# Sliding-window attention: values of two query blocks in one run of matmuls, exponentials of 1024 columns

## The chip, the cores and the metric

The kernel runs on one core of a Trainium2 chip. The metric is the device time of one execution in microseconds (us). The kernel before takes 730.66 us (median of three runs, 730.52 to 731.07). The engines of the core are named as in the profile: PE (TensorE, matmuls) with PEld (its weight loads), DVE (VectorE), ACT (ScalarE), POOL (GpSimd) and SP (SyncE, which issues all transfers here).

## The reference

Attention with 32 heads of 16 dimensions and a causal window of 256 keys stands beside an MLP on the same normalised input, and the output gates one with the other:

```python
xn = layernorm(x)                                  # x: 2048 tokens x 512
q, k, v = split(xn @ wqkv)                         # 32 heads x 16
scores = q k^T * 16 ** -0.5
mask = (i - j >= 0) & (i - j < 256)
s = softmax(where(mask, scores, -1e9)) @ v @ wo
h = gelu(layernorm(xn) @ w1 + b1)                  # 512 -> 1792
g = silu(h @ w2 + b2)
out = x + s * g
```

## The kernel before, in words

**Tiling.** The 2048 tokens are 16 blocks of 128 (qb for queries, kb for keys). The heads are done four at a time: 8 head groups n, so 128 steps of one block of one head group. A query block sees three key blocks: its own (lower triangle), the one before (whole) and the one two before (upper triangle, strict). Products that need precision are made of three products of a high and a low part.

**Slots.** The main loop (line 926) runs over slots t. The slots from -16 to -1 make the inputs ready. Slot t from 0 to 127 does, for step t = 16n + kb: the scores with keys as rows and queries as columns (`prob_block`, line 615, once for each pair of heads p), their exponential on ACT, and two selections on POOL that clear the triangles. It also does the values of step t - 1 (`pv_step`, line 637), and the row maxima of step t + 12 (`LEAD`), which are subtracted through extra rows of q and k before the exponential.

**Scores and exponentials.** One `prob_block` writes 384 columns (its key block against three query blocks) for two heads in two PSUM banks, the tile `stb`, and one ACTIVATE of 2 x 384 = 768 columns reads them. There is one such tile, so the next scores wait until that exponential has ended. In the last 12 slots, where no maxima are left to make, the tile `xy` serves in turn with it.

**Maxima.** `max_block` (line 562) writes the scores of a query block against the block before and its own into `xy` (256 columns for each of four heads), and `first_scores` (line 553) those against the block two before into `zo` (128 columns each). DVE copies the latter over the masked part of the own block (COPY_PREDICATED, 512 elements), and one TENSOR_REDUCE of 1024 elements gives the maxima. `max_rows` (line 584) turns four blocks of them into rows and sends them to the extra rows of q by way of DRAM.

**Values.** `pv_step` multiplies three key blocks' probabilities by v for four heads, each head in a column group of 32 of the PE array, into `otb`, 128 columns of the second bank of `zo`. Each such fp32 matmul is two records in the trace, so a step is 24 records. ACT, in 20 slots DVE, copies `otb` to `oraw`; every fourth step a transfer of 256 KB sends it to DRAM.

**Filling work.** Between these stand units of other matmuls, in the banks `fb`: projections of q, k and v for later head groups, and the first products of the MLP. `tandem` (line 499) makes two jobs run at once, one on the upper and one on the lower 64 rows of the PE array, in two phases between which the two banks change rows. A unit is a pair of matmuls of 512 columns (256 for v). A tandem of q and k has 24 units over five or six slots. Its two results are copied out by ACT at the slot that ends it. `places` deals the units to slots (t, 0) and (t, 1), before and after the slot's second `prob_block`.

**Order.** All engines run their instructions in the order of the program. That order is written by hand: `fills` (units), `plan` by `at(t, ...)` (splits, casts, transfers within a slot), `ends` by `behind(t, ...)` (at a slot's end), and a few tables by slot number such as `MAX_BEHIND` (line 912). Transfers within the slots are issued by SP in that order too. A slot is, in PE's order: scores of p = 1; maxima scores; units; scores of p = 0; units; first scores of the next step; values of the step before.

Of the kernel before, what the change touches and what calls it, by code (L numbers as in the profile page):

```python
# [9 lines left out]
F32 = mybir.dt.float32  # L10
# [40 lines left out]
def mixer_kernel(ctx, tc, x, wqk, wv, wo, w1, b1, w2, b2, out):  # L51
# [12 lines left out]
    pp = attn.enter_context(tc.tile_pool(name="pp", bufs=8))  # L64
# [119 lines left out]
    otb = zo[:, 1, 256:384]  # L184
# [30 lines left out]
    mhalf = const.tile([P, 4], F32, name="mhalf")  # L215
    negc = const.tile([P, 1], F32, name="negc")
# [7 lines left out]
    nc.vector.memset(negc, NEG)  # L224
    mask = upper.bitcast(I32).unsqueeze(1).unsqueeze(1).to_broadcast([P, 2, 2, P])
    neg = negc.unsqueeze(2).unsqueeze(2).to_broadcast([P, 2, 2, P])
    b1s = const.tile([P, NF], F32, name="b1s")
    scales = const.tile([P, 512], F32, name="scales")
# [57 lines left out]

    stage = {}
# [3 lines left out]
    IN_PLACE = (LEAD,)  # L291
# [174 lines left out]
    taken, ends_pair = set(), set()  # L466
# [32 lines left out]
    def tandem(t0, t1, one, two, mid=None, back=None):  # L499

        n = one[0]
        lo, hi = slice(0, 64), slice(64, P)
        mid = mid or max(1, (t0 + t1 + 1) // 2)
        most = n // 4

        def places(slots, last):

            last = min(most, n // (len(slots) + 1)) if last else 0  # L510
            cuts = [(n - last) * k // len(slots) for k in range(len(slots) + 1)]
            out = []
            for t, a, b in zip(slots, cuts, cuts[1:]):
                ahead = min(b - a, n // 3) if t < 16 * NQ - LEAD else min(b - a, max(most, (b - a + 1) // 2))
                out += [(t, 0)] * ahead + [(t, 1)] * (b - a - ahead)
            return out + [(t1, 0)] * last

        first, second = places(range(t0, mid), False), places(range(back or mid, t1), True)
        for phase, where in enumerate((first, second)):
            for i in range(n):  # L520
                flags = dict(start=(phase == 0 and i == 0), stop=(phase == 1 and i == n - 1), skip_group_check=True)
                def unit(i=i, phase=phase, flags=flags):
                    made = ((two if phase == 0 else one)[1](fb[1 - phase], i, hi, **flags),
                            (one if phase == 0 else two)[1](fb[phase], i, lo, **flags))
                    if phase == 1 and i == 0 and t0 < 16 * NQ - LEAD:
                        for r in made:
                            tc.add_manual_dep(r.ins, outs["copy"].ins.name, ORDER, reason="the banks change rows")
                fills.setdefault(where[i], []).append((unit, ()))
        fills.setdefault((t1, 0), []).append((one[2], (fb[0], t1, nc.scalar.copy)))
        if t1 >= 16 * NQ - LEAD:  # L530
            fills[t1, 0].append((two[2], (fb[1], t1, nc.vector.tensor_copy)))
            return
        ends_pair.add(t1)

        def copy(dst, src):
            outs["second"] = nc.scalar.copy(dst, src)
        fills.setdefault((t1, int(t1 + 1 < 16 * NQ - LEAD)), []).append((two[2], (fb[1], t1, copy)))
# [15 lines left out]
    def first_scores(n, qb):  # L553

        slot = slots[n % 2]
        for p in range(2):
            for a in (1, 0):
                r = slice(64 * a, 64 * a + 64)
                nc.tensor.matmul(zo[:, a, P * p: P * (p + 1)], slot[r, 0, p, P * qb: P * (qb + 1)],
                                 slot[r, 1, p, P * (qb - 2): P * (qb - 1)], start=True, stop=True)  # L560

    def max_block(n, qb, ahead=False):

        slot = slots[n % 2]
        if qb % 4 == 0:
            mts[n, qb // 4] = small.tile([P, 2, 2, 4], F32, tag="mt", name=f"mt_{n}_{qb}")
        lo = max(qb - 1, 0)
        off = 128 * (lo + 1 - qb)
        for p in range(2):
            for a in (1, 0):  # L570
                r = slice(64 * a, 64 * a + 64)
                nc.tensor.matmul(xy[:, a, 256 * p + off: 256 * (p + 1)], slot[r, 0, p, P * qb: P * (qb + 1)],
# [869 lines left out]
```

## Time and profile before

| | |
|---|---|
| median of three runs | 730.66 us (730.52 to 731.07) |
| span of the profiled execution | 729.3 us |
| granted TensorE clock | 0.999 |
| PE | 718.0 us busy, 7584 matmul records |
| DVE | 496.2 us busy |
| ACT | 427.6 us busy |
| POOL | 324.1 us busy |

Busy time is the union of an engine's instructions. In a row of the grouped views, the numbers behind the bar are the busy time in us and the mean ns of one instruction, then the idle time of the engine just before them and what ended it. A row of the timeline has the start in us, the duration in us, the engine, the operation, output <- inputs, the shape and how many instructions were merged. Starts of matmuls are recorded, their ends are modelled, and matmuls overlap in the pipeline, so the distance from one start to the next is read rather than the duration. All instructions carry line 43, a helper's, so groups are told apart by tile names: `stb` scores for the exponentials, `pt` probabilities, `zo<-pt` values, `xy` and `zo<-qk` maxima scores, `fb` units, `mt` maxima.

### The profile page before, as it was taken

What the parts mean: (1) busy time and instruction counts of PE and PEld (TensorE: products, weight loads), DVE (VectorE), ACT (ScalarE), POOL (GpSimd) and SP (SyncE); (2) the same over time, 40 slices, a digit from 0 to 9 for tenths busy, and PEclk for the clock granted to TensorE, in tenths of its full rate; (3) what the DMA queues carried; (4) which work ended last, traced back from release to release, by engine and by line L of the source; (5) the groups of instructions that cost most, each with busy time, mean ns of one, the idle gap of its engine ahead of it and who ended that gap; (6) DMA issues with size and microseconds to landing.
All of it is one profiled execution on the core that took longest, in us unless ns stands there. A gap on an engine that the chain in (4) does not pass through costs nothing.

```text
span 729.3 us, 19068 instructions
## 1 busy us (share of the span) xinstructions
PE 718.0 (98%) x7584; PEld 586.6 (80%) x7584; DVE 496.2 (68%) x730; ACT 427.6 (59%) x724; POOL 324.1 (44%) x683
## 2 busy tenths in 40 slices
PE   8999999999999999999999999999999999999997
PEld 8998777777778887777776788888888888888886
DVE  7886776877766777777882656446687856667823
ACT  8767777877777676888878735232344734541001
POOL 7444767767677665777877540203203000001102
PEclk9999999999999999999999999999999999999999
DMA  8324447777776733667624367347223312263701
GB/s 295 81 49 110 100 122 182 219 227 225 199 198 181 209 122 98 161 167 205 179 92 162 104 230 217 129 131 244 87 58 116 117 58 87 68 192 108 249 19 58
DMA packets 61528, 106.77 MB, mean 146 GB/s; under 512 B 12096, under 2 KB 12352, under 8 KB 61440
## 3 DMA queue, kind: packets, MB, share of 16 engines
q1 hardware_dynamic: 61440, 105.56, 49.2%
q8 instruction: 60, 0.98, 0.6%
q14 instruction: 28, 0.23, 0.1%
HBM read 54.53 MB, written 33.82 MB: 121 GB/s over the span
## 4 chain that ended last, share of the span: by engine, by line
PE 93%; ACT 3%; DVE 1%; DMA 1%; SPq 1%; issue 1%; POOL 0%; DVEq 0%; POOLq 0%
PE acc L43 21%; PE fb L43 20%; PE zo L43 14%; PE p L43 9%; PE stb L43 9%; PE s L43 6%; PE h L43 6%; PE xy L43 5%; ACT pt L43 2%; PE pv L43 2%; DVE xy L43 1%; SPq L43 1%; DMA x<-in_x_dram 1%; DVE mt L43 0%; PE tr L43 0%
## 5 line engine op out<-in xcount | busy, mean ns | idle before, releaser
L43 POOL TENSOR_SCALAR_AFFINE_SELECT pt<-pt 128x256 f32<-128x256 f32 x480 | 193.7, 428 | 95.5 <-ACT pt L43 89.4
L43 ACT ACTIVATE pt<-stb 128x768 f32<-128x768 f32 (+1 forms) x244 | 188.8, 774 | 43.2 <-PE stb L43 36.9
L43 DVE TENSOR_REDUCE mt<-xy 128x4 f32<-128x1024 f32 (+1 forms) x128 | 152.6, 1192 | 4.4
L43 DVE COPY_PREDICATED xy<-upper,zo 128x512 f32<-128x512 int32 x112 | 77.9, 695 | 72.1 <-PE xy L43 65.3
L43 POOL TENSOR_TENSOR xo<-xo,gated 128x512 f32<-128x512 f32 x15 | 20.0, 1332 | 221.3 <-DVE gated L43 220.3
L43 PE MATMUL zo<-pt,vt 128*17 128x128 f32 x2880 | 103.7, 275 | 0.0
L43 PE MATMUL fb<-xnT,wqb 64*128 64x512 f32 (+2 forms) x732 | 100.3, 381 | 0.1
L43 PE MATMUL stb<-qk 64*128 64x384 f32 (+1 forms) x488 | 94.6, 382 | 4.6 <-ACT pt L43 2.9
L43 PE MATMUL acc<-w,gh 128*128 128x512 f32 x320 | 98.6, 389 | 0.0
L43 PEld LDWEIGHTS stb<-qk 64*128 64x128 f32 x488 | 45.7, 183 | 48.2 <-ACT pt L43 39.6
L43 PEld LDWEIGHTS zo<-pt,vt 128*17 128x17 f32 x2880 | 67.5, 97 | 15.0 <-issue 4.6
L43 PEld LDWEIGHTS acc<-w,gh 128*128 128x128 f32 x320 | 60.1, 188 | 12.5
L43 PEld LDWEIGHTS fb<-xnT,wqb 64*128 64x128 f32 (+1 forms) x732 | 62.6, 185 | 6.7 <-DVE xy L43 0.3
L43 PE MATMUL acc<-w,gl 128*128 128x512 f32 x160 | 62.2, 389 | 0.0
L43 PE MATMUL xy<-qk 64*128 64x256 f32 (+2 forms) x536 | 57.7, 289 | 0.2 <-DVE mt L43 0.2
L43 PE MATMUL p<-xnT 128*128 128x512 f32 x189 | 51.8, 389 | 0.0
L43 ACT COPY oraw<-zo 128x128 f32<-128x128 f32 x108 | 28.8, 266 | 37.4 <-PE zo L43 28.8
L43 PEld LDWEIGHTS xy<-qk 64*128 64x128 f32 x536 | 46.7, 185 | 4.8 <-issue 2.2
L43 ACT ACTIVATE gated<-acc 128x512 f32<-128x512 f32 x16 | 8.7, 596 | 61.9 <-DVE acc L43 61.9
L43 PE MATMUL s<-wos,ohl 128*128 128x512 f32 (+1 forms) x204 | 44.3, 376 | 0.0
L43 PEld LDWEIGHTS s<-wos,ohl 128*128 128x128 f32 x204 | 36.8, 188 | 7.1
L43 PEld LDWEIGHTS p<-xnT 128*128 128x128 f32 x189 | 35.5, 188 | 7.4
(207 smaller groups left out, 1195.5 us busy)
## 6 DMA issues: line engine op xcount, KB each, us to landing
qk<-sh SPq DMA_DIRECT2D x128, 128.0 KB
qk<-pjr SPq DMA_DIRECT2D x64, 128.0 KB
oT_d<-oraw SPq DMA_DIRECT2D x32, 256.0 KB
w_d<-in_w_dram SPq DMA_DIRECT2D x14, 512.0 KB
xt_d<-xnT SPq DMA_DIRECT2D x12, 512.0 KB
x<-in_x_dram SPq DMA_DIRECT2D x16, 256.0 KB
w<-w_d SPq DMA_DIRECT2D x16, 256.0 KB
or<-oT_d SPq DMA_DIRECT2D x16, 256.0 KB
```

The source lines that it names most:

```text
L43: r = issue(*args, **kwargs)
```

## The change

Two slots become one pair u (slots 2u and 2u + 1, key blocks kb and kb + 1 with kb even).

- **Scores** (`prob_part`): three parts per pair, each of 2 x 512 columns with one exponential of 1024. Parts 0 and 1 hold, for head pair p = 0 or 1, key block kb against three query blocks (384 columns) and key block kb + 1 against its own (128). Part 2 holds key block kb + 1 against the two later query blocks (256) for both head pairs. POOL's selections become one of 512 elements and one of 256 for parts 0 and 1, one of 512 for part 2. Seven buffers of 2 x 512 replace eight of 2 x 384.
- **Values** (`pv_part`): once per pair, into 256 columns, with moving operands of 256, 128, 256 and 128 columns; 32 records instead of 2 x 24. One copy of 256 columns, always on ACT, and one transfer of 128 KB per pair.
- **Maxima**: `xy` now holds the two blocks at the ends of the window, own and two before, and `zo` the middle one. DVE overwrites in `xy`, and reduces middle and ends apart (two reductions of 512). `max_rows` joins them with one more small operation on DVE. In the even slot the order is end scores, middle scores, copy, middle reduction, end reduction; in the odd slot the middle scores and their reduction stand behind the scores of part 2, and the end scores behind two thirds of the units.
- **Units**: every tandem now begins at an even slot and takes all of its slots evenly, all ahead of the second place; between the phases PE drains and counts a semaphore, for which the second phase's first unit waits. The second copy of a tandem stands behind the next part 0.
- **Around it**: some steps of the plan move by one or two slots; the scales live in the space of `wa` and are loaded a third time after the slots; `first_h(1)` is multiplied by them later, on POOL; one piece of x is loaded to another pool.

The core of the diff (`max_ends` keeps the old way for the first two blocks of a head group):

```diff
-    pp = attn.enter_context(tc.tile_pool(name="pp", bufs=8))
+    pp = attn.enter_context(tc.tile_pool(name="pp", bufs=7))
...
-    otb = zo[:, 1, 256:384]
+    otb = zo[:, 1, 256:512]
+    mids = zo[:, :, 0:256].rearrange("q a (p k) -> q a p k", p=2)
+    ends_of = xy.rearrange("q a (p e k) -> q a p e k", p=2, e=2)
...
+    def mark():
+        nc.tensor.drain().then_inc(rows_done, 1)
+        marks[0] += 1
+    def follow(made):
+        for r in made:
+            r.wait_op(rows_done, marks[0], "sem-ge")
...
+        def places(slots):
+            cuts = [n * k // len(slots) for k in range(len(slots) + 1)]
+            return [(t, 0) for t, a, b in zip(slots, cuts, cuts[1:]) for _ in range(b - a)]
+        first, second = places(range(t0, mid)), places(range(back or mid, t1 + 1))
...
+                    if phase == 0 and i == n - 1:
+                        mark()
+                    if phase == 1 and i == 0:
+                        follow(made)
...
+        else:
+            fills.setdefault((t1, 2), []).append((two[2], (fb[1], t1, nc.scalar.copy)))
...
+        own = ends_of[:, :, :, 1]
+        outs["max"] = nc.vector.copy_predicated(own, mask, ends_of[:, :, :, 0]),
+        return lambda: nc.vector.tensor_reduce(out=mt, in_=own, axis=AX.X, op=ALU.max, negate=True)
+    def max_middle(n, qb):
+        if qb < 2:
+            return
+        _, mu = max_places(n, qb)
+        for p in range(2):
+            for a in (1, 0):
+                max_scores(mids[:, a, p], n, qb, a, p, lambda row: row[:, P * (qb - 1): P * qb])
+        nc.vector.tensor_reduce(out=mu, in_=mids, axis=AX.X, op=ALU.max, negate=True)
...
+        if part < 2:
+            w = min(384, S - P * kb)
+            for a in (1, 0):
+                scores(128, a, part, kb, kb, w)
+            for a in (1, 0):
+                scores(0, a, part, kb + 1, kb + 1, 128)
+            w += 128
+        else:
+            w = 512
+            for p in range(2):
+                for a in (1, 0):
+                    scores(256 * p, a, p, kb + 1, kb + 2, 256)
+        outs["exp"] = nc.scalar.activation(pt[:, :, 0:w], both[:, :, 0:w], AF.Exp, scale=DH ** -0.5)
...
+        seq = [(kb, lambda j: pts[u, j // 2][:, j % 2, 128:384], 0, 256),
+               (kb + 1, lambda j: pts[u, j // 2][:, j % 2, 0:128], 128, 256)]
+        if kb:
+            seq[:0] = [(kb - 1, lambda j: pts[u - 1, 2][:, j % 2, 256 * (j // 2): 256 * (j // 2 + 1)], 0, 256),
+                       (kb - 2, lambda j: pts[u - 1, j // 2][:, j % 2, 384:512], 0, 128)]
...
+        oraw = sgp.tile([P, 256], F32, tag="or", name=f"oraw_{u}", bufs=2)
+        outs["copy"] = nc.scalar.copy(oraw, otb)
...
+    for u in range(end // 2):
+        t = 2 * u
+        prob_part(u, 1)
+        rest = own_max(max_ends, t + LEAD)
+        own_max(max_middle, t + LEAD)
+        rest()
+        fill_in(t, 0)
+        planned(t)
+        fill_in(t, 1)
+        ended(t)
+        t += 1
+        prob_part(u, 2)
+        own_max(max_middle, t + LEAD)
+        todo = fills.get((t, 0), [])
+        n = sum(fn.__name__ == "unit" for fn, _ in todo)
+        now[:] = t, 0
+        run(delayed.pop((t, 0), ()))
+        for fn, args in todo[:n - n // 3]:
+            fn(*args)
+        planned(t)
+        fill_in(t, 1)
+        own_max(max_ends, t + LEAD)()
+        for fn, args in todo[n - n // 3:]:
+            fn(*args)
+        if t + 1 < end:
+            prob_part(u + 1, 0)
+        fill_in(t, 2)
+        pv_part(u)
+        own_rows(t + LEAD, t)
+        ended(t)
```

More of the change, by code (lines that the diff above doesn't have):

```diff
@@ L503, in tandem @@
         n = one[0]
[L504 to L518, printed above, removed]
+        lo, hi, box = slice(0, 64), slice(64, P), []
+        mid = mid or (t0 + t1 + 1) // 2
+        def places(slots):
+            cuts = [n * k // len(slots) for k in range(len(slots) + 1)]
+            return [(t, 0) for t, a, b in zip(slots, cuts, cuts[1:]) for _ in range(b - a)]
+        first, second = places(range(t0, mid)), places(range(back or mid, t1 + 1))
         for phase, where in enumerate((first, second)):
@@ L556, in first_scores @@
         for p in range(2):
             for a in (1, 0):
[L558 to L568, printed above, removed]
+                max_scores(ends_of[:, a, p], n, qb, a, p,
+                           lambda row: row.rearrange("d (b k) -> d b k", k=P)[:, qb - 2: qb + 1: 2])
```

213 lines of the change are left out of this document (106 added, 107 removed).

## The prediction

> **What bounds the kernel now.** I read the page's head and its chain first, then the windows by stage, the waits of TensorE, and last the timeline of one slot.
>
> ```profile
> span 729.3 us, 19068 instructions
> PE 718.0 (98%) x7584; PEld 586.6 (80%) x7584; DVE 496.2 (68%) x730; ACT 427.6 (59%) x724; POOL 324.1 (44%) x683
> PE 93%; ACT 3%; DVE 1%; DMA 1%; SPq 1%; issue 1%; POOL 0%; DVEq 0%; POOLq 0%
> ```
>
> TensorE (PE) is busy 98% of the span and is 93% of the chain that ended last, so only what shortens PE's own queue counts. But ends of matmuls are modelled, so bubbles hide in "busy"; I look for them between starts.
>
> ```profile
> core 0: us, PE busy (x) PEld busy (x) DVE busy (x) ACT busy (x) POOL busy (x), PEclk, DMA share, GB/s
> 0.00:63.00 63.00, 60.87 (x660) 56.46 (x662) 49.81 (x93) 47.85 (x87) 32.06 (x64) 1.00 0.51 142
> 63.00:380.00 317.00, 311.81 (x5010) 248.15 (x5008) 234.15 (x291) 241.61 (x409) 226.33 (x534) 1.00 0.61 166
> ```
>
> The slots that the change rewrites run from about 60 to 416 us; in 317 us of them ACT works 242 and DVE 234, both near three quarters. The clock is 1.00 throughout.
>
> ```profile
> PEld stb L43 <- ACT pt L43: 39.6, 150, 0.8
> PE stb L43 <- ACT pt L43: 2.9, 10, 0.4
> PE stb L43 <- DMA qk<-mT_d: 0.6, 1, 0.6
> ```
>
> The weight loads of the probability scores (stb) wait for an exponential 150 times, but mostly the matmuls ahead cover it. DMA hardly holds PE.
>
> ```profile
> 304.45 0.34 PE L43 MATMUL stb<-qk 64*128 64x384 f32 x2
> 304.62 0.34 PE L43 MATMUL zo<-qk 64*128 64x128 f32 x4
> 304.88 0.85 PE L43 MATMUL zo<-pt,vt 128*17 128x128 f32 x24
> 305.69 0.44 PE L43 MATMUL stb<-qk 64*128 64x384 f32 x2
> 305.97 0.40 PE L43 MATMUL xy<-qk 64*128 64x256 f32 x4
> 306.20 1.11 PE L43 MATMUL fb<-xnT,wqb 64*128 64x512 f32 x8
> 307.13 0.35 PE L43 MATMUL stb<-qk 64*128 64x384 f32 x2
> 307.32 0.38 PE L43 MATMUL zo<-qk 64*128 64x128 f32 x4
> 307.63 0.85 PE L43 MATMUL zo<-pt,vt 128*17 128x128 f32 x24
> 308.41 0.44 PE L43 MATMUL stb<-qk 64*128 64x384 f32 x2
> ```
>
> Start to start, this is one slot. Two row halves run at once, so x2 is one pair: 0.23 us for 512 columns (four units in 306.20 to 307.13), 0.12 for 256 (xy), 0.17 for 384 (304.45 to 304.62), hence some 0.06 for 128. That line goes through nothing fixed. Around the values (zo<-pt) it does not hold. Two pairs of 128 before them take 0.26 rather than 0.12: 0.14 to get in.
>
> ```profile
> 65.89 0.41 PE L43 MATMUL zo<-pt,vt 128*17 128x128 f32 x8
> ...
> 68.84 0.63 PE L43 MATMUL zo<-pt,vt 128*17 128x128 f32 x16
> ...
> 379.24 0.41 PE L43 MATMUL zo<-pt,vt 128*17 128x128 f32 x8
> ```
>
> Eight records more cost 0.22, so 24 are 0.66; from 307.63 to 308.41 it is 0.78, 0.12 to get out. The first scores behind take 0.28 (305.69 to 305.97) rather than 0.17, 0.11 more. **One block of values costs 0.37 us beside its columns.** The rows 65.89 and 379.24 are the same block of two head groups 112 slots apart: 313.35/112 = 2.80 us a slot. Without any wait a slot with four units is 0.28+0.23+0.93+0.17+0.26+0.78 = 2.65.
>
> **The change, part by part.** Durations for the other engines:
>
> ```profile
> L43 ACT ACTIVATE pt<-stb 128x768 f32<-128x768 f32 x214 | 174.0, 813 | 38.2 <-PE stb L43 32.1
> L43 ACT ACTIVATE pt<-stb 128x512 f32<-128x512 f32 x15 | 9.0, 599 | 2.7 <-PE stb L43 2.7
> L43 DVE TENSOR_REDUCE mt<-xy 128x4 f32<-128x1024 f32 x120 | 147.1, 1226 | 4.1
> L43 DVE TENSOR_REDUCE mt<-xy 128x4 f32<-128x512 f32 x8 | 5.5, 694 | 0.3
> L43 DVE COPY_PREDICATED xy<-upper,zo 128x512 f32<-128x512 int32 x112 | 77.9, 695 | 72.1 <-PE xy L43 65.3 <-PE zo L43 5.1 <-ACT oraw L43 0.7
> L43 ACT COPY oraw<-zo 128x128 f32<-128x128 f32 x108 | 28.8, 266 | 37.4 <-PE zo L43 28.8 <-POOL mh L43 2.3 <-DVE mT L43 1.9
> L43 ACT COPY vt<-fb 128x256 f32<-128x256 f32 x5 | 1.7, 376 | 3.0 <-PE fb L43 3.0
> L43 ACT COPY pjr<-fb 128x512 f32<-128x512 f32 x26 | 15.3, 590 | 2.8 <-PE fb L43 1.2 <-PE stb L43 0.6
> L43 DVE COPY oraw<-zo 128x128 f32<-128x128 f32 x20 | 5.8, 290 | 1.9 <-PE zo L43 0.5
> L43 DVE TENSOR_TENSOR wqb<-wqkr,wqb 128x512 fp32r<-128x512 f32 x7 | 5.4, 767 | 0.0
> L43 POOL TENSOR_TENSOR hr<-hr,scales 128x512 f32<-128x512 f32 x6 | 7.9, 1345 | 11.0 <-DMA hr<-h_d 11.0
> ```
>
> 1. *Values once per two slots.* 128 blocks become 64: 64 x 0.37 = **-23.7**. Columns stay: 6x128 per slot before, (256+128+256+128) x 2 passes per pair now. Scores stay 1536 columns per pair in six pairs of matmuls instead of four; by the straight line that is 0. [...]
>
> 2. *A pair of slots, hand-timed from the first score pair at 0.* Scores of p=1 (384 and 128 columns) 0.28+0.06 = 0.34; end scores to 0.57; middle scores to 0.69; four units to 1.62; scores of part 2 (two pairs of 256) to 1.85; the odd middle scores to 1.97; three units to 2.67; end scores to 2.90; a unit to 3.13; scores of the next p=0 to 3.36; in 0.14, values 1.32, out 0.12: 4.94 against 2 x 2.65 = 5.30.
>
> ```profile
> 304.83 0.81 ACT L43 ACTIVATE pt<-stb 128x768 f32<-128x768 f32 x1
> 305.85 0.27 ACT L43 COPY oraw<-zo 128x128 f32<-128x128 f32 x1 [0.21 <-PE zo L43]
> 306.17 0.82 ACT L43 ACTIVATE pt<-stb 128x768 f32<-128x768 f32 x1
> 306.46 0.70 DVE L43 COPY_PREDICATED xy<-upper,zo 128x512 f32<-128x512 int32 x1 [0.86 <-PE xy L43]
> ```
>
> 3. *Exponentials.* 256 columns more cost 813-599 = 214 ns, so 1024 take 1.03; three per pair are 3.08 against 4 x 0.813 = 3.25. An exponential starts 0.48 after its scores (305.69, 306.17), here 0.54, and ends at 1.57. PE wants the buffer at 1.62, but a released buffer is used 0.05 later (305.64, 305.69), and a load that had to wait costs the 0.11 again: 1.73, a wait of 0.1. The exponential of the next p=0 lies under the values (1.32), where today's lies under 0.66. Waits today: 2.80 less 2.65 is 0.15 a slot, about 20 us in 128 slots (extra units and the shorter first blocks nearly cancel). New ones of this kind: 0.1 x 64 behind part 1, perhaps 0.14 x 64 elsewhere in the pair, 15. I take **-5**, between -15 (PE always covers) and +5.
>
> 4. *Middle maxima.* The reduction of 1024 (1226) becomes two of 512 (2 x 694); the in-place end block has copy 695 and reduction 694. VectorE's order in an even slot is copy, middles, ends. The end scores start at 0.34, the copy 0.49 later (305.97, 306.46), 0.83 to 1.53; middles to 2.22, ends to 2.91. The odd slot's middle scores overwrite the middles: allowed at 2.22+0.05+0.11 = 2.38, wanted at 1.85+0.1 = 1.95. **A new wait of 0.4**; behind it in PE's queue stand the odd slot's units, end scores and the next scores. Slots with more than four units and phase ends fill part of it; I take 0.3. It is there in 51 pairs (58 pairs still prepare maxima, 7 begin a head group and have no middles): **+15.3**, between 0 and 51 x 0.42 = 21. The odd reductions end well under the values: 0.
>
> 5. *Drains.* 22 row changes of the fill banks now drain PE and count a semaphore, where the first unit used to wait for the values' copy. Nothing in the trace shows a drain; the nearest rows are a matmul's 0.39 less its 0.23 of streaming (1.11 for four units in 0.93) plus the 0.11 of a late load, 0.27 each: 6 at most, 0 at least. 18 stand at the end of an even slot, where items 3 and 4 make PE wait anyway: **+1.5**.
>
> 6. *Copies on ScalarE.* All value copies are now there, 64 of 376 instead of 108 of 266 (and 20 on DVE). At 20 pair ends both bank copies (590 each) and this one stand in a row ahead of the next exponential, and the even middle scores share a bank with the values. With the second copy ahead, the values' copy ends about 0.4 later than PE wants that bank; item 4's wait absorbs most: 0.15 x 20 = **+3**, between 0 and 8. [...]
>
> 7. *The rest.* Before the slots ten blocks have middles: 10 x 0.16 on DVE, 49.81 of 63.00 busy, half exposed: **+0.8** (0 to 2). Selects on GpSimd cover the same elements in 5 instead of 8 instructions, and the values now come a part later: 0. Values leave in 64 transfers rather than 32, 32 more issues on SyncE that nobody waits for: 0. The third load of the scales and one multiply on GpSimd stand under the first matmuls after the slots: 0; uncovered 1.3 for the multiply and the load beside it.
>
> Sum: -23.7 -5 +15.3 +1.5 +3 +0.8 = -8.1. The profiled execution spans 729.3, 1.4 under the median of 730.66; I take the change off the median: **722.6**.
>
> **The rivals.** *PE alone decides (20%).* If PE comes to the odd middle scores no earlier than VectorE, because of the 0.1 waits, drains and extra units, item 4 is nil: 722.6-15.3 = 707.3, with item 3's own waits there some 709. For it: DVE has 25% idle. Against it: the hand schedule misses by 0.4.
>
> *VectorE sets the pace (20%), slower.* Its work per pair grows from 3.84 to 4.17, and any further instruction of it ahead of the even middles (a 0.77 subtraction of a weight, a transpose) adds wholly to PE's wait. It decides from a wait of 0.3+8.1/51 = 0.46 per pair; at 0.6 it is 722.6+15.3 = 737.9. For it: the three in a row are serial and PE's other work there is fixed. Against: nearly nothing else runs on DVE before the last third.
>
> *The waits only move (13%).* If the exponentials cost as much waiting as today and a little more (item 3 at +3 instead of -5), the time is 730.6. For it: three long links on one buffer. Against: the longest cover, the values, doubles.
>
> That fewer blocks are issued is fixed by the program; that each costs 0.37 was seen with and without a wait ahead.
>
> **How the numbers follow.** The forecast itself has 47% (716 to 729). With PE alone 20%, moved waits 13%, VectorE 20%, the range 708 to 735 leaves out the far half of the last and the tail below the first. 0.2% (1.5 us) is about what a measurement of this kernel can tell. Faster 67%, same 13%, slower 20%.
>
> **What would show it.** Right: 64 blocks of 32 records, the 0.14, 0.12 and 0.11 once each per pair; exponentials of 1.03; pairs near 5.4 where four units stand in each slot; PE's load for the odd middle scores waiting for a DVE reduction. Wrong: pairs near 5.05 (PE alone) or above 5.6 (VectorE), 256-column passes of values that take other than 0.22, or drains over 0.3.

## The result

| | before | after |
|---|---|---|
| median of four runs each | 730.85 us (730.52 to 731.07) | 741.04 us (738.69 to 742.74) |
| profiled execution, span | 729.3 us | 737.0 us |
| ratio after / before | | 1.0137, 95% interval 1.0115 to 1.0158 |

The change makes the kernel 1.4% slower: 10.2 us by the medians, 7.7 us by the two profiled spans. The forecast was 722.6 us, faster, with 735 us as the upper end of its range. It is wrong in sign and out of its range.

The head of the page of the kernel after, and the chain that ended last:

```profile
span 737.0 us, 17546 instructions
PE 714.8 (97%) x6848; PEld 574.2 (78%) x6848; DVE 504.4 (68%) x854; ACT 408.5 (55%) x608; POOL 302.8 (41%) x500
PE 87%; ACT 4%; DVE 3%; DMA 2%; issue 2%; SPq 1%; POOL 1%; ACTq 0%; DVEq 0%; POOLq 0%
```

TensorE has 736 records fewer, yet its share of the chain fell from 93% to 87%: waits for ScalarE, VectorE and transfers have come in. The windows by stage, and a third one around the worst place:

```profile
core 0: us, PE busy (x) PEld busy (x) DVE busy (x) ACT busy (x) POOL busy (x), PEclk, DMA share, GB/s
63.00:380.00 317.00, 302.77 (x4276) 230.85 (x4276) 232.28 (x390) 219.78 (x301) 201.69 (x364) 0.99 0.63 164
296.00:312.00 16.00, 13.34 (x160) 9.95 (x160) 9.96 (x16) 8.96 (x12) 9.08 (x16) 0.89 0.65 159
```

In the same 317 us of the slots TensorE is busy 303 us instead of 312, and its clock is no longer 1.00 throughout. Half of the pairs of slots still take 5.5 us or less, near what was drawn by hand. One of them in the timeline of TensorE, start to start:

```profile
203.11 0.51 PE L43 MATMUL stb<-qk 64*128 64x384 f32 x4 [0.59 <-ACT pt L43]
203.45 0.45 PE L43 MATMUL xy<-qk 64*128 64x256 f32 x4
203.86 0.44 PE L43 MATMUL zo<-qk 64*128 64x128 f32 x4
204.14 1.13 PE L43 MATMUL fb<-xnT,wqb 64*128 64x512 f32 x8
205.11 0.39 PE L43 MATMUL stb<-qk 64*128 64x256 f32 x4
205.34 0.38 PE L43 MATMUL zo<-qk 64*128 64x128 f32 x4
205.56 0.90 PE L43 MATMUL fb<-xnT,wqb 64*128 64x512 f32 x6
...
206.77 0.41 PE L43 MATMUL stb<-qk 64*128 64x384 f32 x4
207.11 1.49 PE L43 MATMUL zo<-pt,vt 128*17 128x256 f32 x32
208.54 0.51 PE L43 MATMUL stb<-qk 64*128 64x384 f32 x4
208.87 0.39 PE L43 MATMUL xy<-qk 64*128 64x128 f32 x4
209.10 1.15 PE L43 MATMUL fb<-xnT,wqb 64*128 64x512 f32 x8
210.33 0.51 PE L43 MATMUL stb<-qk 64*128 64x256 f32 x4
```

From 203.11 to 208.54 are 5.43 us; the forecast said near 5.4 where four units stand in each slot. But a look inside shows other terms than it named. The two places with middle scores take 0.28 (203.86 to 204.14) and 0.22 us (205.34 to 205.56), where 0.12 were drawn, and no wait of the forecast's 0.3 stands at the second. That the sum of this pair agrees is luck in part. And the pairs are not all like this one. By the starts of the values' blocks, the 56 pairs from 66.93 to 386.09 us take 5.70 us on average, against two slots of 2.80 before. The longest is this, again in TensorE's timeline:

```profile
298.28 1.49 PE L43 MATMUL zo<-pt,vt 128*17 128x256 f32 x32
299.70 0.50 PE L43 MATMUL stb<-qk 64*128 64x384 f32 x4
302.78 0.44 PE L43 MATMUL xy<-qk 64*128 64x128 f32 x4 [2.58 <-DMA qk<-pjr]
...
304.27 0.69 PE L43 MATMUL stb<-qk 64*128 64x256 f32 x4
304.74 1.50 PE L43 MATMUL fb<-xnT,wqb 64*128 64x512 f32 x6
```

TensorE waits 2.58 us for the low parts of q and k of the next head group (`qk<-pjr`). Behind the wait the clock falls, to 0.50 from 304.5 to 307.5 us: six unit records take 1.50 us, above (205.56) 0.90. The waits of TensorE over the whole span:

```profile
PE stb L43 <- ACT pt L43: 3.8, 9, 0.7
PE xy L43 <- DMA qk<-pjr: 2.6, 1, 2.6
PE stb L43 <- DMA qk<-mT_d: 2.5, 2, 2.1
PE xy L43 <- DVE mt L43: 1.9, 4, 0.8
```

The second and third are about rows of head groups that arrive late: before, `xy` had no such wait, and that for `qk<-mT_d` was 0.6 us. In the part of the forecast on bounds stood "DMA hardly holds PE".

### The profile page after: what moved, and what is told of

Its sections match the earlier page's. It is cut to its first block, busy times and chain, and to the rows that moved or that the text cites. A ratio compares the mean times of both kernels' runs of the same rounds, so it can differ in the third digit from the quotient of the medians.

```text
span 737.0 us, 17546 instructions
## 1 busy us (share of the span) xinstructions
PE 714.8 (97%) x6848; PEld 574.2 (78%) x6848; DVE 504.4 (68%) x854; ACT 408.5 (55%) x608; POOL 302.8 (41%) x500
## 4 chain that ended last, share of the span: by engine, by line
PE 87%; ACT 4%; DVE 3%; DMA 2%; issue 2%; SPq 1%; POOL 1%; ACTq 0%; DVEq 0%; POOLq 0%
PE acc L43 20%; PE fb L43 18%; PE zo L43 13%; PE p L43 9%; PE stb L43 7%; PE s L43 6%; PE h L43 6%; PE xy L43 5%; ACT pt L43 2%; PE pv L43 2%; DVE mt L43 1%; SPq L43 1%; DVE xy L43 1%; DMA qk<-pjr 1%; DMA qk<-mT_d 1%
## 5 line engine op out<-in xcount | busy, mean ns | idle before, releaser
L43 ACT ACTIVATE pt<-stb 128x1024 f32<-128x1024 f32 (+1 forms) x176 | 177.7, 1010 | 72.5 <-PE stb L43 65.2
L43 POOL TENSOR_SCALAR_AFFINE_SELECT pt<-pt 128x512 f32<-128x512 f32 (+1 forms) x296 | 163.5, 573 | 124.4 <-ACT pt L43 123.9
L43 DVE COPY_PREDICATED xy<-upper,xy 128x512 f32<-128x512 int32 x112 | 77.8, 694 | 71.4 <-PE xy L43 71.3
L43 POOL TENSOR_TENSOR xo<-xo,gated 128x512 f32<-128x512 f32 x15 | 20.0, 1331 | 220.1 <-DVE gated L43 219.0
L43 PE MATMUL fb<-xnT,wqb 64*128 64x512 f32 (+2 forms) x732 | 106.1, 390 | 1.2 <-POOL sv L43 1.0
L43 PE MATMUL acc<-w,gh 128*128 128x512 f32 x320 | 98.7, 389 | 1.1 <-ACT gh L43 1.1
L43 DVE TENSOR_REDUCE mt<-xy 128x4 f32<-128x512 f32 (+1 forms) x128 | 92.3, 721 | 2.3
L43 PE MATMUL zo<-pt,vt 128*17 128x128 f32 (+1 forms) x1920 | 90.6, 328 | 0.0
L43 PE MATMUL stb<-qk 64*128 64x384 f32 (+1 forms) x704 | 79.3, 302 | 8.4 <-ACT pt L43 3.8
L43 PEld LDWEIGHTS stb<-qk 64*128 64x128 f32 x704 | 57.5, 186 | 36.2 <-ACT pt L43 18.5
L43 DVE TENSOR_REDUCE mt<-zo 128x4 f32<-128x512 f32 x112 | 76.3, 682 | 1.2 <-PE zo L43 0.7
L43 PEld LDWEIGHTS zo<-pt,vt 128*17 128x17 f32 x1920 | 49.1, 97 | 32.2 <-issue 0.6
L43 PEld LDWEIGHTS acc<-w,gh 128*128 128x128 f32 x320 | 60.0, 188 | 13.8 <-ACT gh L43 1.5
L43 PEld LDWEIGHTS fb<-xnT,wqb 64*128 64x128 f32 (+1 forms) x732 | 62.2, 188 | 7.1 <-POOL sv L43 1.1
L43 PE MATMUL xy<-qk 64*128 64x256 f32 (+2 forms) x544 | 59.0, 294 | 4.7 <-DMA qk<-pjr 2.6
L43 PE MATMUL acc<-w,gl 128*128 128x512 f32 x160 | 62.4, 390 | 0.0
L43 PEld LDWEIGHTS xy<-qk 64*128 64x128 f32 x544 | 45.7, 186 | 12.7 <-issue 4.6
L43 PE MATMUL p<-xnT 128*128 128x512 f32 x189 | 51.8, 389 | 0.0
L43 PE MATMUL zo<-qk 64*128 64x128 f32 x448 | 44.1, 274 | 0.9 <-DVE mt L43 0.2
L43 PE MATMUL s<-wos,ohl 128*128 128x512 f32 (+1 forms) x204 | 44.3, 376 | 0.0
L43 ACT ACTIVATE gated<-acc 128x512 f32<-128x512 f32 x16 | 8.7, 596 | 61.9 <-DVE acc L43 61.9
L43 PEld LDWEIGHTS s<-wos,ohl 128*128 128x128 f32 x204 | 36.8, 188 | 7.1
```

The costliest lines, as they stand in the source:

```text
L43: r = issue(*args, **kwargs)
```

## The experiments

The theories. **1, late rows:** the spans in which q, k and the maxima of the next head group are produced were moved, their transfers come later in SyncE's one ordered queue, and TensorE waits and then runs slow. **2, VectorE's pace:** the wait at the middle maxima. **3, prices:** drains and short matmul steps cost more than forecast, a block of values less.

| kernel | median us | ratio to before | 95% interval |
|---|---|---|---|
| after | 741.04 | 1.0137 | 1.0115 to 1.0158 |
| rows6 | 742.11 | 1.0149 | 1.0136 to 1.0162 |
| mids2 | 738.85 | 1.0100 | 1.0084 to 1.0116 |
| nocp | 736.23 | 1.0069 | 1.0056 to 1.0082 |
| split | 771.85 | 1.0557 | 1.0544 to 1.0571 |
| first | 736.34 | 1.0072 | 1.0050 to 1.0094 |
| oact | 747.35 | 1.0220 | 1.0207 to 1.0233 |
| oact_mids | 739.07 | 1.0109 | 1.0096 to 1.0122 |
| split1 | 762.42 | 1.0436 | 1.0416 to 1.0456 |
| first_nocp | 733.29 | 1.0022 | 1.0004 to 1.0040 |
| drain2 | 746.88 | 1.0217 | 1.0204 to 1.0230 |
| tail | 740.85 | 1.0139 | 1.0125 to 1.0153 |
| best1 | 732.54 | 1.0025 | 1.0015 to 1.0035 |
| before_rows | 735.45 | 1.0066 | 1.0052 to 1.0081 |
| before_short | 737.26 | 1.0084 | 1.0071 to 1.0097 |
| best2 | 730.02 | 0.9991 | 0.9982 to 0.9999 |

Differences between kernels below are differences of ratios times 731 us.

### Late rows: rows6, first, oact, before_rows

**rows6**

```diff
-                               ((76, 81), (82, 87)), ((88, 93), (94, 99))), 2):
+                               ((76, 79), (80, 87)), ((88, 93), (94, 99))), 2):
```

> One change to the kernel after: the rows of head group 6 (its q and k columns after the rotation) are produced at slots 76-79 and 80-87, not 76-81 and 82-87. In the kernel after the group's q and k columns left SyncE at 299.24 us, against 291.17 before, and TensorE waited 2.74 us for them at 299.98 and then ran at half speed for a stretch. Theory 1 (rows that arrive late): this wait goes, with the slow stretch behind it: 3 to 7 us less than the kernel after, so 734 to 738 us, and the pair that took 9.17 us takes 5.5. Theory 2 (VectorE's pace) and theory 3 (drains, and a values block that is cheaper than 0.37 us): within 1 us of the kernel after, since the pairs lose time everywhere and a late row only moves the wait.

Measured: no gain (+0.9 us by the ratios, within the intervals). The wait at 300 us is gone, as theory 1 said, but the time is not. TensorE's waits in the slots of this kernel:

```profile
PE stb L43 <- DMA qk<-mT_d: 5.1, 3, 3.1
```

Waits for the maxima rows (`qk<-mT_d`), 2.5 us in the kernel after, are 5.1 here. So the wait moved to the next late transfer, and one span alone is not the cause. SyncE's issues in the kernel after show what these rows stand behind:

```profile
157.56 1.19 SPq L43 DMA_DIRECT2D qk<-pjr  x2
158.84 0.56 SPq L43 DMA_DIRECT2D mT_d<-mT  x1
159.45 0.56 SPq L43 DMA_DIRECT2D xt_d<-xnT  x1
160.05 0.61 SPq L43 DMA_DIRECT2D wqkr<-in_wqk_dram  x1
160.76 0.76 SPq L43 DMA_DIRECT2D oT_d<-oraw  x1
161.62 0.59 SPq L43 DMA_DIRECT2D qk<-qk  x1
162.30 2.50 SPq L43 DMA_DIRECT2D qk<-sh  x4
164.90 1.43 SPq L43 DMA_DIRECT2D qk<-pjr  x2
166.43 0.55 SPq L43 DMA_DIRECT2D qk<-mT_d  x1
```

Each issue takes SyncE some 0.6 us, and the queue has no gap over 0.2 us. The maxima rows were written out at 158.84, but they are read in at 166.43, behind seven issues for a group that is needed later. TensorE waits for them from 166.47 (168.56 less 2.09):

```profile
166.08 0.39 PE L43 MATMUL fb<-xnT,wqb 64*128 64x512 f32 x2
168.56 0.50 PE L43 MATMUL stb<-qk 64*128 64x384 f32 x4 [2.09 <-DMA qk<-mT_d]
```

**first** (with the edit of rows6)

```diff
-            behind(t + 2, bring_in)
+            at(t + 2, bring_in)
```

> Two changes to the kernel after: the rows of head group 6 are produced at slots 76-79 and 80-87 (as in the run before this one, which by itself brought nothing: the wait at 300 us went, and waits of 2.0 to 3.3 us for the maxima rows stood at 166 and 306 us instead), and SyncE issues the reading-in of the maxima rows at the front of its slot, ahead of the q and k columns of that slot, not behind them. Theory 1 (rows late through SyncE's one ordered queue): with both waits gone and the slow stretch behind each, 4 to 9 us less than the kernel after, 732 to 737 us, and no wait of TensorE on a DMA over 0.5 us between 66 and 385 us. Rival (the late rows are only where a loss shows that VectorE and the blocks make): the waits move once more, 739 to 743 us.

Measured: 4.8 us less than the kernel after, 736.3 us, as theory 1 said. TensorE's wait for `qk<-mT_d` fell to 1.0 us (one place, at 360 us), above the 0.5 that I had set; the wait for `qk<-pjr` is gone. Not all of the gain is the waits themselves: the granted clock was 0.996 to 1.000 in these runs, 0.992 to 0.998 in those of the kernel after. Span times granted clock, an estimate of the time at full clock, is 736.1 us (median) for the kernel after and 733.2 for first, so that some 3 of the 4.8 us are left without the clock.

**oact**

```diff
-        at(2 * u + 2, nc.sync.dma_start, oT_d[n, :, :, cols].rearrange("j r t -> (j r) t"), oraw)
+        nc.scalar.dma_start(oT_d[n, :, :, cols].rearrange("j r t -> (j r) t"), oraw)
```

> One change to the kernel after: the 64 transfers that carry the values' results out are issued by ScalarE right behind its own copy, not by SyncE, so that SyncE has 64 issues of some 0.55 us and its 49 us of waits for that copy less. ScalarE gets about 64 x 0.1 to 0.6 us more. Theory 1 (SyncE's queue makes the rows late; the forecast had put its 32 more transfers at 0): the waits on rows at 166 and 300 us shrink or go, 4 to 8 us less than the kernel after, 733 to 737 us. Theory 2 (VectorE's pace): within 1 us of the kernel after. If ScalarE's issues hold up the exponentials, up to 64 x 0.3 us more, 741 to 760 us.

Measured: 6.1 us more than the kernel after. The expectation of theory 1 failed; that ScalarE's issues hold up the exponentials (741 to 760 us) held. SyncE had 64 issues less, and the waits stayed:

```profile
PE stb L43 <- ACT pt L43: 5.9, 15, 0.7
PE xy L43 <- DMA qk<-qk: 2.9, 1, 2.9
PE stb L43 <- DMA qk<-mT_d: 2.4, 1, 2.4
```

So the result transfers in SyncE's queue are not what makes rows late; by rows6 and first, it is where the rows' own transfers stand. The added time is ScalarE's: TensorE waits for its exponentials in 15 places rather than 9, and the weight loads of the scores wait for them 31.0 us in 73 places rather than 17.1 in 43 (66 to 385 us).

**before_rows**, the suspected cause alone, in the kernel before:

```diff
-                               ((75, 79), (80, 85)), ((86, 91), (92, 97))), 2):
+                               ((76, 81), (82, 87)), ((88, 93), (94, 99))), 2):
...
-    for f, *span in ((6, 98, 103), (8, 104, 109), (10, 110, 115), (12, 116, 121, 118, 119), (2, 122, 127, 124, 125)):
+    for f, *span in ((6, 100, 105), (8, 106, 111), (10, 112, 115), (12, 116, 121, 118, 119), (2, 122, 127, 124, 125)):
```

(and the loads and splits of the first weights as in the kernel after)

> The kernel before with the kernel after's later spans for the rows of head groups 6 and 7 (76-81, 82-87, 88-93, 94-99) and for the unit pieces and weight loads that follow them; nothing else of the change. If late rows cost by the spans alone: a wait of TensorE on q and k columns near 300 us and 2 to 6 us more, 733 to 737 us. If they cost only because SyncE's queue is fuller and the slots are passed otherwise in the kernel after: within 1 us of the kernel before, 730 to 732 us.

Measured: 4.5 us more than the kernel before by the medians, as expected if the spans cost by themselves. The wait for the rows is there:

```profile
299.20 0.44 PE L43 MATMUL xy<-qk 64*128 64x128 f32 x4 [1.48 <-DMA qk<-pjr]
```

It explains 1.5 of the 4.5 us. Slot 75 has no units here, which may cost another part; that was not separated.

### VectorE: mids2, nocp, first_nocp

**mids2**: the middle scores two units later (the odd slot alike)

```diff
         rest = own_max(max_ends, t + LEAD)
...
+        for fn, args in todo[:2]:
+            fn(*args)
         own_max(max_middle, t + LEAD)
         rest()
-        fill_in(t, 0)
+        for fn, args in todo[2:]:
+            fn(*args)
```

> One change to the kernel after: the scores of the middle blocks (whose maximum is taken apart, into the bank of the values) are put two unit pieces later in both slots, so that VectorE has some 1.5 us more to read the end blocks' scores before them. Theory 2 (the wait for VectorE at the middle maxima, 0.3 us in each of 51 pairs): 8 to 15 us less than the kernel after, 726 to 733 us. Theory 1 (late rows): the wait is not there to be removed, so within 2 us of the kernel after, 739 to 743 us. Theory 3 (drains and cheap values blocks): within 2 us of the kernel after as well, or slower by up to 5 us if the pieces now change the form of the matmuls once more (some 0.1 us in each of 51 pairs, twice).

**nocp**

```diff
-        outs["max"] = nc.vector.copy_predicated(own, mask, ends_of[:, :, :, 0]),
+        if 16 * n + qb < LEAD:
+            outs["max"] = nc.vector.copy_predicated(own, mask, ends_of[:, :, :, 0]),
```

> One change to the kernel after: from the block of index LEAD on, VectorE's predicated copy of the own block's scores is left out (some 0.2 to 0.3 us of VectorE for each of the blocks), so the maxima from there on are taken without the mask. It leaves this part of the computation out. Theory 2 (VectorE sets the pace): VectorE is quicker by 0.4 us in each pair, and the time falls by 8 to 20 us, to 721 to 733 us. Theory 1 (late rows) and theory 3: VectorE isn't waited for, so within 3 us of the kernel after, 738 to 743 us.

Measured: 2.7 us less for mids2 and 5.0 us less for nocp, between the expectations of theories 1 and 2. The row of the copy in the kernel after, and the wait in its slots (66 to 385 us):

```profile
L43 DVE COPY_PREDICATED xy<-upper,xy 128x512 f32<-128x512 int32 x112 | 77.8, 694 | 71.4 <-PE xy L43 71.3
```

```profile
PEld zo L43 <- DVE mt L43: 5.1, 14, 0.7
```

VectorE is waited for, by the weight loads of the middle scores, but for some 5 us and not 15. In nocp the copy is gone from all but ten of its 112 blocks, 102 x 0.694 = 71 us of VectorE, and the kernel gained a fourteenth of that. (The expectation took 0.2 to 0.3 us for one copy; the row has 0.694.)

**first_nocp** (the edits of first and of nocp)

> The kernel after with its rows in time (rows of head group 6 two slots earlier, maxima rows read in at the front of the slot: 736.3 us by itself, against about 742 for the kernel after in the same kind of comparison) and, besides, without the predicated copy of the own block on VectorE from the block of index LEAD on, so that the maxima from there are taken without the mask. In the kernel after, leaving the copy out brought 5 us. If the wait for VectorE at the middle maxima and the late rows are two causes that add: 736.3 - 5 to - 8, 728 to 731.5 us. If the time saved on VectorE was the same time as that of the rows: 735 to 737 us.

Measured: 733.3 us, 3.7 us less than first. The gains of the two causes add to a good part: 4.8 + 5.0 alone, 8.4 together.

### Prices: split, split1, drain2, before_short

**split** and **split1**: `pv_part(u, 0)` issues the first 16 of a pair's 32 records of values in split, the first 8 in split1

```diff
+        if u % 8:
+            pv_part(u, 0)
         if t + 1 < end:
             prob_part(u + 1, 0)
         fill_in(t, 2)
-        pv_part(u)
+        pv_part(u, 1 if u % 8 else None)
```

> One change to the kernel after: the values matmuls of a pair are issued as two blocks of 16 with the next pair's first exponential's scores and the unit pieces of the last third between them, instead of one block of 32. The matmuls are the same; each pair has one block of values more (56 more in all less 7). The forecast priced one block at 0.37 us (0.14 to get in, 0.12 to get out, 0.11 for the first score load). By that price: +18 us, 759 us. Theory 3 (a block costs much less, since part of what was seen at its edges is the rate of short matmuls): +5 to +12 us, 746 to 753 us. Theory 1 says nothing against the price: 755 to 762 us. Below 745 us a block would cost next to nothing and the change has no gain to lose.

> The kernel after with the values of a pair in two blocks, as in the earlier split, but with only a quarter of the matmuls (8 of 32) in the first block, so that the other 24 still cover the exponential that the next scores wait for. In the earlier split (16 and 16) 18.0 of the 30.8 us were waits of the scores for that exponential, which leaves 0.26 us for each of 49 added blocks. Price of a block 0.26 us: +12 to +14 us over the kernel after, 753 to 755 us, with the waits for the exponential at 3 to 6 us. The forecast's 0.37 us: +18 us, 759 us. Under 0.15 us: below 749 us.

Measured: 30.7 us and 21.9 us more than the kernel after, for 56 blocks more (7 of 8 pairs). Both above what I expected. TensorE's timeline of split shows one such pair end:

```profile
205.63 0.40 PE L43 MATMUL fb<-xnT,wqb 64*128 64x512 f32 x2
205.96 0.84 PE L43 MATMUL zo<-pt,vt 128*17 128x256 f32 x16
206.73 0.50 PE L43 MATMUL stb<-qk 64*128 64x384 f32 x4
207.16 0.84 PE L43 MATMUL zo<-pt,vt 128*17 128x256 f32 x16
208.35 0.50 PE L43 MATMUL stb<-qk 64*128 64x384 f32 x4 [0.34 <-ACT pt L43]
```

A unit in front of the values takes 0.33 rather than 0.23: 0.10 to get in. The block takes 0.77 for half of 1.32: 0.11 to get out. The scores behind it take 0.43 against 0.34 (206.77 to 207.11 in the kernel after): 0.09. That is 0.30 for a block. The second block takes 1.19, 0.42 more than the first, for its scores wait for the exponential that 32 matmuls used to cover. The view's 18.0 us for these waits (49 times, named in the expectation of split1) stand against 3.5 us of the same kind in the slots of the kernel after, so 14.5 were added: 30.7 - 14.5 = 16.2 are left, 0.29 for each of the 56. In split1 the same waits are 4.6 us, 1.1 more, which leaves 20.8, or 0.37 for each. But its timeline shows 0.30, too, and besides an exponential that is not quite covered:

```profile
205.55 0.63 PE L43 MATMUL zo<-pt,vt 128*17 128x256 f32 x8
206.11 0.50 PE L43 MATMUL stb<-qk 64*128 64x384 f32 x4
206.54 1.06 PE L43 MATMUL zo<-pt,vt 128*17 128x128 f32 x24
207.73 0.50 PE L43 MATMUL stb<-qk 64*128 64x384 f32 x4
```

The first block takes 0.56 for 0.44, the scores behind it 0.43 again. The second takes 1.19, where its columns are 0.88 and getting out 0.11: 0.20 more, which the view of waits does not list. So a block costs some 0.30 us; the forecast's 0.37 is what split1 gives when nothing is taken off for that.

The 0.14 to get in belongs in part to the two pairs of 128 columns themselves: in the kernel after they take 0.22 and 0.28 us with a unit behind them, and no values. Summed over the starts of 112 slots, less the straight line, the lag in front of the values is 17.6 us before. In the same slots after, it is 5.8, but the middle scores with a unit behind them lag 11.9 us more in 98 places. That is 17.7 together: of this part nothing was gained. Why these pairs lag was not separated.

**drain2**

```diff
-                    if phase == 0 and i == n - 1:
+                    if phase == 0 and i in (n // 2 - 1, n - 1):
                         mark()
```

> One change to the kernel after: each tandem of unit pieces has one drain of TensorE more, after half of its first phase (22 more of them). The forecast took 0.07 us for a drain (1.5 us for 22, bounds 0 and 6). In the trace of the kernel after, a unit piece and the score behind it stand 0.48 us apart over a drain and 0.23 without. If that is all exposed: 22 x 0.25 = 5.5 us, 746 to 748 us. By the forecast: +1.5 us, 742 to 743.5 us.

Measured: 5.9 us more for 22 drains, 0.27 us each. The forecast had 0.27 as its upper bound and took a quarter of it. The 22 drains of the kernel after show the same in its timeline above: four units take 0.97 us to the scores of part 2 without a drain (204.14 to 205.11), and 1.23 with one (209.10 to 210.33). At all 22 places the last units lag 0.24 to 0.44 us behind the straight line (0.04 in the first of the two, without a drain), 7.0 in all, so none of them is hidden.

**before_short**

```diff
-            nc.tensor.matmul(both[:, a, 0:w], slot[r, 1, p, P * kb: P * (kb + 1)],
-                             slot[r, 0, p, P * kb: P * kb + w], start=True, stop=True)
+            nc.tensor.matmul(both[:, a, 0:min(w, 256)], slot[r, 1, p, P * kb: P * (kb + 1)],
+                             slot[r, 0, p, P * kb: P * kb + min(w, 256)], start=True, stop=True)
+        for a in (1, 0) if w == 384 else ():
+            r = slice(64 * a, 64 * a + 64)
+            nc.tensor.matmul(both[:, a, 256:w], slot[r, 1, p, P * kb: P * (kb + 1)],
+                             slot[r, 0, p, P * kb + 256: P * kb + w], start=True, stop=True)
```

> The kernel before with the scores of each exponential (384 columns) issued as 256 and 128 columns: 224 more pairs of matmuls, the same columns, no other change. By the forecast's straight line (0.06 us for 128 columns, nothing fixed) nothing: 730.5 to 731.5 us. If a short step has a fixed part of 0.03 to 0.06 us where it follows another short one: 224 x 0.03 to 0.06, 7 to 13 us more, 738 to 744 us. The change itself adds some 110 such steps to the scores, so that half of what is measured here stands in the kernel after.

Measured: 6.3 us more by the medians for 224 steps, 0.028 us each, a little under the lower end. TensorE's matmuls wait for exponentials no more than before (2.8 us in 9 places, against 2.9 in 10), so the time is in the steps: the straight line is not free of a fixed part. The change adds two such steps to the scores of each of 64 pairs: 128 x 0.028 = 3.6 us, as an estimate, that the forecast put at 0.

### Together: oact_mids, tail, best1, best2

**oact_mids** (the edits of rows6, first, mids2 and oact)

> All of them at once on the kernel after: rows of head group 6 two slots earlier, the maxima rows read in at the front of the slot, the results' transfers issued by ScalarE, and the middle scores two unit pieces later. If the two causes add (late rows 5 to 8 us, VectorE's wait at the middle maxima 5 to 10 us), 723 to 731 us, at or below the kernel before. If it is one cause that shows in two places, 733 to 737 us, no better than the best of the single edits.

Measured: 739.1 us. Against oact it is 8.1 us less, so the three edits together are worth about that, but ScalarE's issues take most of it again. The expectation had not counted them.

**tail**: `den = fetch_sums()` ahead of `fetch_scales(0, scales)`

> One change to the kernel after, behind the last values: SyncE issues the four transfers that read the denominators ahead of the transfer that reads the scales once more. In the kernel after they were issued from 426.37 us, behind the scales at 425.50, for which SyncE stood still for 4.8 us; in the kernel before from 419.20. From the first projection to the first output score it took 1.8 us longer than before, and the values ended sooner against it. If this order is the cause: 1 to 3 us less, 738 to 740.5 us. If the multiplication by the scales that GpSimd now has there is: no change, 741 to 743 us.

Measured: no change. The order of these transfers is not the cause. What is, the two rows of the last hidden block on ScalarE show, first before and then after:

```profile
420.22 0.72 ACT L43 ACTIVATE hf<-hf,b1s 128x512 f32<-128x512 f32 x1 [0.44 <-DVE hf L43]
```

```profile
431.55 0.72 ACT L43 ACTIVATE hf<-hf,b1s 128x512 f32<-128x512 f32 x1 [5.96 <-POOL hf L43]
```

The activation waits for GpSimd's multiplication. It starts 6.7 us behind the first projection after the slots (424.87), where it was 0.9 behind it (419.29).

**best1** (rows6, first, mids2 but for slots 17 and 103, tail)

> Four edits of the kernel after together: rows of head group 6 two slots earlier, maxima rows read in at the front of the slot, middle scores two unit pieces later in both slots (but for slots 17 and 103, where the values then waited for the maxima), denominators read in ahead of the scales. Against about 742 for the kernel after: rows -5.5, VectorE's wait -4 to -8, tail -1 to -2: 727 to 731 us, level with the kernel before or up to 0.5% below it. If the causes overlap: 733 to 736 us.

Measured: 732.5 us, 8.2 us less than the kernel after, 0.25% over the kernel before. That is short of the expectation of causes that add (727 to 731). VectorE's wait at slot 17 stayed (1.15 us at 112 us).

**best2** (as best1 without the edit of tail; slots 16 and 102 excepted too; the last hidden block scaled as before)

```diff
+    def open_again():
+        mlp["scales"] = pp.tile([P, 2, 512], F32, tag="pt", name="scales_1")
+        fetch_scales(0, mlp["scales"][:, 0])
+    at(126, open_again)
...
-            nc.vector.tensor_copy(ready[f], fb[f])
+            nc.vector.tensor_mul(ready[f], fb[f], mlp["scales"][:, 0])
...
-    nc.gpsimd.tensor_tensor(ready[1], ready[1], scales, op=ALU.mult)
```

> The kernel after with rows of head group 6 two slots earlier, maxima rows read in at the front of the slot, middle scores two unit pieces later (but for slots 16, 17, 102 and 103), and the last hidden block scaled by VectorE as in the kernel before, from a second load of the scales into a free buffer of the probabilities, so that GpSimd's multiplication in the tail is gone. Against 732.5 us for the version before it: the tail 0 to -2, the wait of the values at 110 and 350 us -1.5: 729 to 732 us. Under 729.5 it beats the kernel before; what is then still lacking to the forecast's 722.6 is drains (4 us more than forecast) and the steps at the edges.

Measured: 730.0 us, ratio 0.9991: within 0.2% of the kernel before, which is no difference that counts. The tail, that is, what follows the slots: from the first projection (`acc`) to the first output score (`s`) in TensorE's timeline it takes 461.61 - 418.09 = 43.52 us, as in the kernel before (462.81 - 419.29), against 470.18 - 424.87 = 45.31 in the kernel after: the tail's 1.8 us came from GpSimd's multiplication and the load ahead of it, for best2 leaves out the one and places the other earlier. The windows of best2 at the places shown above:

```profile
63.00:380.00 317.00, 304.64 (x4360) 231.31 (x4356) 242.58 (x400) 223.91 (x307) 206.11 (x372) 1.00 0.62 166
296.00:312.00 16.00, 15.57 (x220) 10.78 (x212) 12.32 (x21) 11.65 (x16) 10.33 (x20) 1.00 0.56 143
```

The clock is 1.00 again, and 84 records more fit into the same 317 us than in the kernel after.

## Why the prediction was wrong

Several steps failed, and each is named here with what the runs showed in its place.

**Item 7 and the part on bounds, late rows.** This step has no number in the forecast. Item 7 lists "the rest" at +0.8. It prices the added transfers (0, and oact bears that out: without them on SyncE the waits stayed). It does not mention that every span in which rows of a head group are produced was moved, nor that the maxima rows are read in behind the columns of that slot. The part on bounds, "DMA hardly holds PE", took a property of the plan for one of the machine. Cost: 4.8 us, by first; 4.5, by before_rows, where 1.5 of it stand in the timeline as the wait.

**Item 5, drains.** +1.5 forecast, 5.9 by drain2, and the kernel after's own 22 drains all stand in its starts. The upper bound was right. That the waits of items 3 and 4 would hide three quarters of them was wrong; those waits are smaller than assumed. +4.4.

**Item 1, values.** -23.7 forecast. Of the 0.37 for a block, the 0.12 to get out and the 0.11 behind were saved as forecast (0.11 each for a block that is left). The 0.14 to get in was not: the middle scores that stood ahead of the values lag with a unit behind them, too, and this makes up for what the fewer blocks save (17.6 and 17.7 us). That is 64 x 0.14 = 9 us less gain. The scores' straight line left out 3.6 us more, 0.028 us for a step by before_short.

**Item 4, middle maxima.** +15.3 forecast. Making VectorE quicker, or asking for the middles later, brought 3 to 5 us. The wait is where it was foreseen, in the odd slot, but it is a third of it; that TensorE comes late there itself, through the steps above, would account for it, which no run singles out. With it falls the rival "VectorE sets the pace". It gave 737.9 us, near the measured time, by a mechanism that is not the one at work. The rival "PE alone decides" had that lateness right and its price wrong: it gave 707, for it left the lateness itself out.

**Item 3, exponentials.** -5 forecast, not tested by a run. The forecast read some 20 us of waits out of 2.80 less 2.65 for a slot. The starts of TensorE's steps show less: in front of scores that waited for an exponential, the time over what such steps take without a wait is between 6 and 7 us in 112 slots, both before and after. So there was no gain, as the rival "the waits only move" had it. Split, where 49 pair ends wait 18.0 us in all once the cover is halved, shows that this chain is close to the bound.

**Item 7, tail.** "Stand under the first matmuls: 0; uncovered 1.3". It was uncovered: 1.8 us.

**Item 6, copies.** +3 forecast. No row before shows the loads of `zo` waiting for a copy of the values. In the kernel after, the loads of the middle scores wait for one in four places, 0.7 us in all (`PEld zo L43 <- ACT oraw L43: 0.7, 4, 0.2`). The same sum in front of steps that waited for a copy of the values gives some 1.4 us. -1.6.

**Adding up.** -8.1 as forecast; rows +4.8, drains +4.4, values +9, steps +3.6, exponentials +5, tail +1.8, middle maxima -10.3 to -12.3, copies -1.6. That gives +6.6 to +8.6, against +7.7 for the profiled execution and +10.2 for the medians. Several of these terms are uncertain by a microsecond or more, so that they meet so closely is luck in part.

The runs of the kernel after spread by 4 us, those of the kernel before by 0.6; the granted clock was 0.998 in the quickest and 0.992 in the slowest. Span times clock is 735.5 us for the quickest and 735.1 for the slowest. By this estimate the spread between them is the clock, and so is most of what the medians lose beyond the profiled execution.

**What was right.** The 0.12 and 0.11 once for each block, 64 blocks of 32 records, exponentials of 1.03 us (1028 ns in the grouped view), pairs near 5.4 us, the load for the odd middle scores waiting for a VectorE reduction. All of it could hold and the sign still be wrong, since the loss sits in late rows, in drains, in the lag of short steps and in the tail.

## What to carry to other kernels

When a change moves steps of a plan, list each moved transfer with the slot that first reads it, and count what stands ahead of it in the issuing engine's queue (here some 0.6 us for each issue): a queue without a gap for 12 us (154.52 to 166.43 in the kernel after) makes "two slots later" into a wait. A price read at an edge (0.37 us around a block) may belong in part to the short steps beside it; price it by adding a block, and look at what the added block uncovers. When a change loses time, put the suspected part alone into the old kernel: before_rows did that in one run.

## What the runs showed of the hardware

- After TensorE's wait of 2.58 us the granted clock was 0.89 over 296 to 312 us. In windows of half a microsecond it is 0.50 from 304.5 to 307.5 us. 0.11 of 16 us is 1.8 us lost, on top of the wait. After the wait of 2.09 us at 166 us, the window from 160 to 176 us has 1.00. In rows6, after a wait of 3.1 us at that place, it has 0.89. Its window from 300 to 316 us has 0.89, too, though no wait for rows there is over 2.0 us (the three of this kernel are 5.1 us together, the longest 3.1). So the length of one wait does not decide alone.
- A drain of TensorE costs 0.27 us, measured by doubling (5.9 us for 22); in the starts of the kernel after it is 0.26 (1.23 less 0.97).
- A step of 128 columns costs 0.028 us beyond its columns when it is split off (6.3 us for 224), and two pairs of 128 columns with a unit behind them took 0.17 to 0.28 us in the kernel after, where the line through 256, 384 and 512 columns gives 0.12.
